# Two of eight batches transposed by TensorE instead of the DMA crossbar, and one expert's weights moved in the load queue

## The chip, the cores and the metric

The kernel runs on one core of a Trainium2 chip. The metric is the device time of one execution in microseconds (us); the times of several executions are given by their median. PE is TensorE's matmul stream and PEld its weight loads; DVE is VectorE, ACT ScalarE, POOL GpSimd, SP SyncE. Every engine works through its own list of instructions in a fixed order and waits, where it must, on semaphores of others. DMA transfers are issued from the queues of POOL, SP and ACT and land later.

## The reference, cut to what matters

```python
# attention: x (8, 8, 512, 64), state (8, 8, 32, 64); batch, head, tokens, width
scores  = scale * x @ state^T          # 512 x 32 for each batch and head
xread   = softmax(scores) @ state
scores2 = scale * state @ x^T          # the same products, the other way round
sread   = softmax(scores2) @ x
attn    = concat([xread, sread], axis=2)          # 544 rows for each batch and head
x       = attn with the heads side by side        # 4352 rows x 512

# mixture of 8 experts, every row through every expert
P = exp(x @ w_gate - max); 8 times: rows normalised, columns normalised, * N / E
out = sum over e of P[:, e] * (relu(x @ w1[e]) @ w2[e])   # w1: 512 x 1024, w2: 1024 x 512
```

Inputs and output are 32-bit floats. The kernel loads `x` and the weights into 16-bit tiles on the way.

## The kernel before, in words

**Two parts.** The first part holds attention for all eight batches, expert 0, the routing (the eight normalisations of P) and the first two blocks of expert 1's first layer. In it, every piece of work is an `op` with a rank, the engines that may run it with their costs, what it comes after, and the buffers that it takes or uses. `issue` (L48) walks through them: again and again it takes the ready op that could start earliest by these costs, then the one of lowest rank, and emits it. So the order of each engine's instructions is fixed when the program is built, from the costs written in the ops; on the chip each engine keeps to it. What `after` names serves this order; on the chip an instruction waits for data and buffers. The second part, the loop over experts 1 to 7 (`layer1`, `layer2`, L226 to L317), is written out in a fixed order.

**Attention, batch by batch.** The input of batch `b` is loaded by two POOL DMAs of 256 KB (L380) into `x_nat`, tokens on partitions; four such buffers rotate, so the load of batch 4 waits until batch 0's is done with. Scores need the input with the width on partitions: `xT`, 16 blocks of 128 x 128 per batch, three buffers. Two crossbar transposes per batch, issued by SP (L457), make it, one for the first four heads and one for the others. A batch then runs in two halves `q` of four heads. For each: PE's scores into the PSUM tile `psB` (L469; there is one such pair of banks, so the next scores wait until it is read); on DVE a flip of it into `eA` (L490), maxima, subtraction; on ACT two exponentials; on DVE sums and products; at last a flip into `aT` (L528), the attention weights that all experts read. Beside it PE transposes the other softmax (L547), that is copied to `ETs`, and PE reads the input with it (`su_ps`, L562). With that read, the `x_nat` buffer comes free.

**Expert 0.** Its two weight matrices are loaded by POOL, two DMAs of 512 KB each (L434). For each batch PE projects the state with w1 into `V` (L662), multiplies `V` by `aT` for the hidden layer (`hps`, L684; needs both halves' `aT`), ReLU goes to ACT or DVE (`hT`, L350 and L352), and PE runs the second layer (`yps`, L719). All of this is interleaved with attention by the planner. Six PSUM banks rotate among transposes, projections, hidden blocks and outputs.

**Routing.** After the last batch's logits, PE and DVE alternate: DVE normalises rows (L624 to L628), PE sums columns (`csb_ps`, L641), DVE normalises columns (L634 to L636). PE's list has expert 0's remaining work between the column sums.

**Queues around the change.** POOL issues, in this order: the identity matrices, then the loads: x 0, expert 0's w1, x 1, expert 0's w2, x 2, x 3, x 4, expert 1's w1, x 5, expert 1's w2, x 6, x 7, later the weights of the experts from 2 on (L166, L168). SP issues half of the state loads, the gate weights, and the 16 crossbar transposes in order of batches. `make_identity` stands twice for the 16-bit identity `identh`. The first PE instructions are 16 transposes of the states (`stT_ps`, L399), then 64 small matmuls for the gate (`G_ps`, L414), then batch 0's scores.

Of the kernel before, what the change touches and what calls it, by code (L numbers as in the profile page):

```python
# [10 lines left out]
FP16 = mybir.dt.float16  # L11
# [78 lines left out]
def kernel(  # L90
# [9 lines left out]
    nc = tc.nc  # L100
# [10 lines left out]
    NSC = S // 128  # L111
    NP = H // 2
    NQ = NP // 2
    NX = B * S
    NJ = NFB // 2
    DH = Dm // 2
# [3 lines left out]

    blocks = [(b * S, S) for b in range(B)] + [(NX, B * Ns)]

# [9 lines left out]
    def bank(shape, dtype, name, tag="bank"):  # L132
        return pools[tag].tile(shape, dtype, name=name, tag=tag)

    aT = persist.tile([128, B, NQ, S], FP16, name="aT")
    xsT = persist.tile([128, NKC, B * Ns], FP16, name="xsT")
# [2 lines left out]
    Pmat = persist.tile([128, NTB, E], FP32, name="Pmat")  # L139

    identh = persist.tile([128, 128], FP16, name="identh")
    make_identity(nc, identh)
    ident32 = persist.tile([128, 128], FP32, name="ident32")
    ones128 = persist.tile([128, 128], FP32, name="ones128")
    wg_st = persist.tile([128, NKC, E], FP32, name="wg_st")
    wgh = persist.tile([128, NKC, E], FP16, name="wgh")
    stT = persist.tile([128, B, NQ, 128], FP16, name="stT")
    G = persist.tile([128, B, NQ, E], FP16, name="G")

# [42 lines left out]
    def project(e, bi):  # L192
        if bi == B:
            return
        w1h = w16[e][0]
        V = vpool.tile([128, NQ, F], FP16, name="V", tag="V")
        vt[(e, bi)] = V
        for f in range(F // 512):
            cols = ds(f * 512, 512)
            ps = [bank([128, 512], FP32, "v_ps", ring[0]) for _ in range(NQ)]  # L200
            for j in range(4):
                for q in range(NQ):
                    r = ((j ^ q) % 2) * 64
# [117 lines left out]
    due_x = lambda u: 6.0 + 4.4 * u  # L321
    due_e = lambda bi: 14.0 + 13.0 * bi
    due_1 = 135.0
    rings = {"bank": Ring(6), "pair": Ring(1)}
    SHY = 0.8
    EVICT16 = {"DVE": (0.34, 0.48), "ACT": (0.48, 0.66)}
# [3 lines left out]
    def op(rank, on, emit, after=(), takes=(), uses=(), also=()):  # L330
        o = Op(rank, on, emit, after, takes, uses, also)
        ops.append(o)
        return o

    def slot(pool, n, shape, dtype, tag):
        return Slot(rings.setdefault(tag, Ring(n)),
                    lambda: pool.tile(shape, dtype, name=tag, tag=tag))

    def psum(shape, dtype, name):
        return Slot(rings["bank"], lambda: bank(shape, dtype, name))  # L340

    def copy(eng, out, in_):
        if eng == "ACT":
            nc.scalar.copy(out=out, in_=in_)
        else:
            engines[eng].tensor_copy(out=out, in_=in_)
# [7 lines left out]
    def dma(rank, kb, emit, after=(), takes=(), uses=(), also=()):  # L354
        return op(rank, {"DMA": (kb / 300.0, kb / 300.0 + 2.2)}, lambda _: emit(), after, takes, uses, also)
# [15 lines left out]
    wgc = op((10.0,), {"DVE": (0.15, 0.25)}, lambda _: nc.vector.tensor_copy(out=wgh, in_=wg_st), [wgd])  # L371


    make_identity(nc, identh)
    xn = [slot(axp, 4, [128, H, NSC * D], FP16, "x_nat") for _ in range(B)]
    x_ready = []
    for b in range(B):
# [5 lines left out]

        x_ready.append(dma((0, 1 + 2 * b), 1024, load, takes=[xn[b]], also={"POOL": 2.0}))

    make32 = op((8.0,), {"POOL": (0.5, 0.6)}, lambda _: make_identity(nc, ident32))
    bd = []
    for s_ in range(2):
# [4 lines left out]
    stT_ready = []  # L393
    for g in range(4):
        ps = psum([128, 4, 128], FP16, "stT_ps")

        def turn(_, g=g, ps=ps):
            for i in range(4):
                nc.tensor.transpose(ps.tile[:, i], st_in[:, 2 * g + i // 2, i % 2].rearrange("p s d -> p (s d)"),  # L399
                                    identh)  # L400

        def keep(eng, g=g, ps=ps):
            copy(eng, stT[:, ds(2 * g, 2)].rearrange("p b q c -> p (b q) c"), ps.tile)

        t = op((0, 1, g), {"PE": (0.35, 0.55)}, turn, bd, [ps])
        stT_ready.append(op((0, 1, g), EVICT16, keep, [t], uses=[ps]))
    gps = [psum([128, B, E], FP32, "G_ps") for _ in range(NQ)]

    def gmul(_):
        for b in range(B):  # L410
            for j in range(4):
                for q in range(NQ):
# [6 lines left out]
                  lambda eng, q=q: copy(eng, G[:, :, q], gps[q].tile), [gm_op], uses=[gps[q]])  # L419
# [4 lines left out]
    w_ready = {}  # L424
    t_ready = []

    def weights_ops(e, rank):
        w1 = slot(mw, 2, [128, NKC, F], FP16, "w1h")
        w2 = slot(mw, 2, [128, NFB, Dm], FP16, "w2h")
        wslots[e] = (w1, w2)  # L430
        for k, (w, n, r) in enumerate(((w1, 2, w1r), (w2, NJ, w2r))):
            def load(w=w, n=n, r=r):
                for g in range(2):
                    nc.gpsimd.dma_start(out=w.tile[:, ds(g * n, n), :], in_=r[e, :, ds(g * n, n), :])  # L434

            w_ready[e, k] = dma(rank[k], 2048, load, [], [w], [], {"POOL": 2.0})

    def w1_ready(e):
        return [w_ready[e, 0]]
# [1 line left out]
    def w2_ready(e):  # L441
        return [w_ready[e, 1]]

    weights_ops(0, [(0, 2), (0, 4)])
    weights_ops(1, [(due_1 - 60.0, k) for k in range(2)])


    a_ready, su_ready, gates = {}, [], []
# [3 lines left out]
    for b in range(B):  # L452
        xT = slot(axt, 3, [128, H * NSC // 2, 128], FP16, "xT")
        xt_ready = []
        for g in range(2):
            def turn(b=b, g=g, xT=xT):
                nc.sync.dma_start_transpose(out=xT.tile[:, ds(8 * g, 8), :],  # L457
                                            in_=xn[b].tile[:, ds(4 * g, 4), :].rearrange("p h c -> p (h c)"))

            xt_ready.append(op((due_x(2 * b - 2), 0, g), {"XBAR": (1.4, 3.0)}, lambda _, turn=turn: turn(),  # L460
                               [x_ready[b]], [] if g else [xT], [xn[b]] + ([xT] if g else [])))
        for q in range(NQ):
            r = lambda n, b=b, q=q: (due_x(2 * b + q) + 0.1 * 5.54 * n,)
            ps = Slot(rings["pair"], lambda: bank([128, 2, 512], FP32, "psB", "pair"))
# [12 lines left out]
            def tokens(t):  # L477
                return t.rearrange("p (i s c) -> p i s c", i=2, s=2)

            o2 = op((due_x(2 * b + q), 0), {"PE": (0.18, 0.38)}, score, [xt_ready[q]] + stT_ready,  # L480
                    [ps], [xT])
            mxA, sA, rA = rows("mxA"), rows("sA"), rows("rA")
            nmB, nsB, rowsum, rrec = small("nmB"), small("nsB"), small("rowsum"), small("rrec")
# [86 lines left out]

            u = op(r(9), {"PE": (0.25, 0.45)}, read, [k2], [su], [ETs, xn[b]])
            su_ready.append(op(r(9), {"DVE": (0.13, 0.25), "ACT": (0.15, 0.30)}, keepS, [u], [], [su]))

    def gate_op(bi, after):
        t0, tn = blocks[bi]
        n = tn // 128
        ps = psum([128, 4, E], FP32, "gate_ps")

        def mul(_):
            for i in range(n):  # L580
                rs = ds(i * 128, 128)
                if bi < B:
                    terms = [(aT[:, bi, q, rs], G[:, bi, q]) for q in range(NQ)]
                else:
                    terms = [(xsT[:, kc, rs], wgh[:, kc, :]) for kc in range(NKC)]
                for k, (lhs, rhs) in enumerate(terms):
                    nc.tensor.matmul(ps.tile[:, i], lhs, rhs, start=(k == 0),
                                     stop=(k == len(terms) - 1))

        t = op((due_x(2 * bi + 2), 0), {"PE": (0.25, 0.45)}, mul, after + G_ready, [ps])  # L590
        return op((due_x(2 * bi + 2), 0), {"DVE": (0.10, 0.20), "ACT": (0.15, 0.30)},
                  lambda eng: copy(eng, logits[:, ds(t0 // 128, n)], ps.tile[:, :n]), [t], [], [ps])
# [5 lines left out]
    rank = (-1.0,)  # L598
# [93 lines left out]
    for bi in range(len(blocks)):  # L692
# [6 lines left out]
        for fb in range(NFB):  # L699
            ps = psum([128, 512], FP32, "hps")  # L700
# [8 lines left out]
            t = op((due_e(bi) + 0.05 * 13.7 * fb,), {"PE": (0.44, 0.62)}, mul, deps, [ps], held)  # L709
# [48 lines left out]
    for bi in range(2):  # L758
# [12 lines left out]
        for j in range(NJ):  # L771
            for i in range(2):
                ps = psum([128, S], FP32, "hps")
# [7 lines left out]
                t = op((due_1 + 5.0 * bi, 1, j, i), {"PE": (0.44, 0.62)}, mul, deps + [got], [ps], held)  # L781
# [91 lines left out]
```

## Time and profile before

| | |
|---|---|
| median of 3 runs | 788.36 us (787.72 to 788.41) |
| profiled execution, its own time | 788.79 us |
| its span | 786.8 us |
| PE busy | 749.1 us, 95% of the span |
| DVE busy | 632.1 us, 80% |
| ACT busy | 524.0 us, 67% |
| POOL busy | 36.8 us, 5% |
| software DMA queue (POOL's loads) | 20.97 MB |
| hardware DMA queue (transposes, output, states) | 13.39 MB |

The span is the time from the first to the last instruction in the trace; the execution's own time has 2.0 us around it. "Busy" is the time in which an engine had an instruction running; matmuls are pipelined, so one that takes 379 ns by its row can start 107 or 213 ns after the one before. A line of the timeline gives start and duration in us, engine, line of the kernel, operation, what is written from what, how many instructions are merged in it, and in square brackets how long the engine stood idle before and who released it. Line numbers in profile lines are those of the kernel before.

### The profile page before, as it was taken

The numbers are of one execution on the slowest core, as the hardware profiler recorded it, in microseconds if no ns is written. First come the engines' busy times: TensorE is split into PE (matmuls) and PEld (weight loads), VectorE is DVE, ScalarE is ACT, GpSimd is POOL, SyncE is SP. The second block draws the span as 40 slices with busy tenths as digits, with TensorE's granted clock in tenths as the row PEclk, the third lists the DMA queues.
The fourth block names the chain that finished last, engine by engine and source line by source line (L and its number), as shares of the span: only waits on it lengthen the run. The fifth ranks groups of instructions, "written<-read, shape, count | busy, mean of one in ns | idle before, by whom it ended". The sixth has DMA issues, their size and how long they took to land.

```text
span 786.8 us, 16245 instructions
## 1 busy us (share of the span) xinstructions
PE 749.1 (95%) x6529; PEld 499.6 (64%) x6529; DVE 632.1 (80%) x1561; ACT 524.0 (67%) x1020; POOL 36.8 (5%) x58
## 2 busy tenths in 40 slices
PE   1699999989999999999999999999999999999996
PEld 1244444556667667766677667766677667766775
DVE  1699977678898888878888888878888888878885
ACT  1687787677767666576657666576667666576662
POOL 5111000100001000010001000010001000000000
PEclk9999999999999999999999999999999999999999
DMA  9999200330004100060004100060004200012223
GB/s 164 186 124 178 21 1 1 56 54 1 1 1 79 31 1 2 1 108 2 1 1 77 33 1 2 1 108 2 1 1 75 35 1 1 2 44 93 94 101 128
DMA packets 45916, 35.67 MB, mean 45 GB/s; under 512 B 21008, under 2 KB 37392, under 8 KB 45840
## 3 DMA queue, kind: packets, MB, share of 16 engines
q0 software_dynamic: 21248, 20.97, 18.1%
q1 hardware_dynamic: 23504, 13.39, 8.6%
q8 instruction: 51, 0.84, 0.4%
q10 hardware_dynamic: 1088, 0.26, 0.2%
q14 instruction: 25, 0.20, 0.1%
HBM read 42.48 MB, written 8.91 MB: 65 GB/s over the span
## 4 chain that ended last, share of the span: by engine, by line
PE 66%; DVE 4%; ACT 1%; issue 0%; DVEq 0%
PE hps L219 23%; PE Bseed L265 17%; PE E L265 11%; PE A L265 11%; PE v_ps L204 3%; DVE acc L279 2%; DVE sm L244 1%; ACT Hm L238 1%; DVE sm L247 0%; DVE Hm L245 0%; DVE T L178 0%; DVE sm L246 0%; DVE acc L287 0%; ACT Bseed L290 0%; DVEq L279 0%
## 5 line engine op out<-in xcount | busy, mean ns | idle before, releaser
L238 ACT ACTIVATE Hm<-hps 128x512 f16<-128x512 f32 (+1 forms) x488 | 261.6, 572 | 182.4 <-PE hps L219 167.3
L265 PEld LDWEIGHTS <-Hm 128*128 128x128 f16 x1904 | 186.1, 98 | 72.0 <-issue 4.1
L219 PE MATMUL hps<-aT,V 128*128 128x512 f16 x864 | 230.6, 379 | 0.0
L279 DVE SCALAR_TENSOR_TENSOR acc<-Bseed,Pmat,acc 128x256 f32<-128x256 f32 x357 | 156.9, 479 | 55.6 <-PE Bseed L265 52.9
L265 PEld LDWEIGHTS <-sm 128*128 128x128 f16 x1428 | 134.3, 98 | 53.1 <-DVE sm L244 24.4
L265 PE MATMUL A<-w2h,Hm 128*128 128x256 f16 x952 | 124.5, 273 | 1.9 <-ACT Hm L350 1.9
L265 PE MATMUL Bseed<-T,Hm 128*128 128x256 f16 x952 | 124.5, 273 | 1.0 <-DVE acc L279 0.8
L219 PEld LDWEIGHTS <-V 128*128 128x128 f16 x864 | 84.5, 98 | 44.5
L208 ACT CAST V<-v_ps 128x512 f16<-128x512 f32 x216 | 111.2, 609 | 0.0
L279 DVE SCALAR_TENSOR_TENSOR acc<-E,Pmat,acc 128x256 f32<-128x256 f32 x238 | 104.3, 477 | 5.2 <-PE E L265 0.9
L719 PE MATMUL yps<-w2h,hT 128*128 128x512 f16 x272 | 67.3, 386 | 0.0
L244 DVE TENSOR_TENSOR sm<-Hm 128x512 f16<-128x512 f16 (+1 forms) x122 | 49.9, 409 | 19.7 <-ACT Hm L238 18.9
L265 PE MATMUL E<-T,sm 128*128 128x256 f16 x476 | 64.4, 274 | 0.7
L279 DVE SCALAR_TENSOR_TENSOR acc<-A,Pmat,acc 128x256 f32<-128x256 f32 x119 | 52.3, 479 | 15.0 <-PE A L265 14.9
L265 PE MATMUL Bseed<-T,sm 128*128 128x256 f16 x476 | 62.4, 273 | 0.4 <-ACT Bseed L290 0.4
L265 PE MATMUL E<-w2h,sm 128*128 128x256 f16 x476 | 62.3, 273 | 0.0
L245 DVE TENSOR_TENSOR Hm<-Hm 128x512 f16<-128x512 f16 (+1 forms) x122 | 50.0, 410 | 4.2
L247 DVE TENSOR_TENSOR sm<-Hm,sm 128x512 f16<-128x512 f16 (+1 forms) x122 | 50.0, 410 | 4.2
L246 DVE TENSOR_TENSOR sm<-sm,Hm 128x512 f16<-128x512 f16 (+1 forms) x122 | 49.1, 402 | 0.0
L290 ACT COPY Bseed<-A 128x512 f32<-128x512 f32 (+1 forms) x63 | 34.5, 548 | 19.5 <-PE A L265 18.9
L719 PEld LDWEIGHTS <-hT 128*128 128x128 f16 x272 | 24.9, 100 | 26.8 <-issue 2.9
L684 PE MATMUL hps<-aT,V 128*128 128x512 f16 x160 | 41.0, 393 | 0.4 <-DVE aT L528 0.4
(100 smaller groups left out, 511.9 us busy)
## 6 DMA issues: line engine op xcount, KB each, us to landing
w1h<-in_moe_w_dram POOLq DMA_DIRECT2D x16, 512.0 KB, 7.1
w2h<-in_moe_w_dram POOLq DMA_DIRECT2D x16, 512.0 KB, 8.3
out_dram<-acc SPq DMA_DIRECT2D x32, 256.0 KB, 2.8
x_nat<-in_x_dram POOLq DMA_DIRECT2D x16, 256.0 KB, 11.9
out_dram<-acc SPq DMA_DIRECT2D x8, 64.0 KB, 1.7
st_st<-in_state_dram ACTq DMA_DIRECT2D x4, 64.0 KB, 3.0
st_st<-in_state_dram SPq DMA_DIRECT2D x4, 64.0 KB, 2.8
xT<-x_nat SPq DMA_TRANSPOSE x16, 12.0
```

Of the source, the lines that this page charges most:

```text
L208: nc.scalar.copy(out=V[:, q, cols], in_=ps[q])
L219: nc.tensor.matmul(out, lhs, rhs, start=(k == 0), stop=(k == len(terms) - 1))
L238: nc.scalar.activation(out=Hm[:, i, j, :tn], in_=hps[:, :tn], func=AF.Relu)
L244: nc.vector.tensor_add(s1, a21, a22)
L245: nc.vector.tensor_sub(a21, a11, a21)
L246: nc.vector.tensor_sub(s2, s1, a11)
L247: nc.vector.tensor_sub(s4, a12, s2)
L265: nc.tensor.matmul(dst[:, c], lhs(j, c), rhs[:, j], start=first and c == 0 and j == 0, stop=(j == NJ - 1), skip_group_check=True)
L279: nc.vector.scalar_tensor_tensor(out=dst, in0=src[:, c], scalar=p[:, k], in1=dst, op0=ALU.mult, op1=ALU.add)
L290: nc.scalar.copy(out=Bb[:, :nk], in_=A[:, :nk])
L684: nc.tensor.matmul(ps.tile[:, :tn], lhs, rhs, start=(k == 0), stop=(k == len(terms) - 1))
L719: nc.tensor.matmul(yps.tile, hT[fb].tile[:, ds(tk * 128, 128)], w2h[:, fb, :], start=(fb == 0), stop=(fb == NFB - 1))
```

## The change

Batches 0 and 1 (`NT = 2`) get their `xT` from PE. For each half of four heads, eight matmuls against the identity transpose 128 x 128 blocks into a PSUM bank, and two copies of 128 x 512 take it to SBUF, on DVE or ACT as the planner chooses. Batches 2 to 7 keep the crossbar; its cost in the planner goes from (1.4, 3.0) to (2.4, 6.0). One of the two `identh` identities goes, and the other becomes an op. Expert 1's weight loads are declared after the scores' transposes of the last batch (`last_x`). Built, the program has them on POOL's queue behind the load of x 7, with no further wait on the transposes; the loads of x 4 to x 7 move up.

```diff
+    NT = 2
 ...
-    make_identity(nc, identh)
 ...
-    make_identity(nc, identh)
 ...
+    makeh = op((0, 1.5), {"POOL": (0.5, 0.6)}, lambda _: make_identity(nc, identh))
 ...
-        t = op((0, 1, g), {"PE": (0.35, 0.55)}, turn, bd, [ps])
+        t = op((0, 1, g), {"PE": (0.35, 0.55)}, turn, bd + [makeh], [ps])
 ...
-            w_ready[e, k] = dma(rank[k], 2048, load, [], [w], [], {"POOL": 2.0})
+            w_ready[e, k] = dma(rank[k], 2048, load, last_x if e else [], [w], [], {"POOL": 2.0})
 ...
-    weights_ops(1, [(due_1 - 60.0, k) for k in range(2)])
 ...
-        for g in range(2):
+        for g in range(2 if b < NT else 0):
+            ps = psum([128, 8, 128], FP16, "xT_ps")
+
+            def turnX(_, b=b, g=g, ps=ps):
+                for k in range(8):
+                    nc.tensor.transpose(ps.tile[:, k], xn[b].tile[:, 4 * g + k // 2, ds((k % 2) * 128, 128)],
+                                        identh)
+
+            def keepX(eng, g=g, k=0, ps=ps, xT=xT):
+                copy(eng, xT.tile[:, ds(8 * g + 4 * k, 4), :], ps.tile[:, ds(4 * k, 4), :])
+
+            t = op((due_x(2 * b + g) - 2.0, 0), {"PE": (0.68, 0.85)}, turnX, [x_ready[b], makeh], [ps], [xn[b]])
+            xt_ready.append([op((due_x(2 * b + g) - 2.0, 0), EVICT16, lambda eng, k=k, keepX=keepX: keepX(eng, k=k), [t],
+                                [] if g + k else [xT], [ps] + ([xT] if g + k else [])) for k in range(2)])
+        for g in range(0 if b < NT else 2):
             def turn(b=b, g=g, xT=xT):
                 nc.sync.dma_start_transpose(out=xT.tile[:, ds(8 * g, 8), :],
                                             in_=xn[b].tile[:, ds(4 * g, 4), :].rearrange("p h c -> p (h c)"))
 
-            xt_ready.append(op((due_x(2 * b - 2), 0, g), {"XBAR": (1.4, 3.0)}, lambda _, turn=turn: turn(),
-                               [x_ready[b]], [] if g else [xT], [xn[b]] + ([xT] if g else [])))
+            xt_ready.append([op((due_x(2 * b - 2), 0, g), {"XBAR": (2.4, 6.0)}, lambda _, turn=turn: turn(),
+                                [x_ready[b]], [] if g else [xT], [xn[b]] + ([xT] if g else []))])
 ...
-            o2 = op((due_x(2 * b + q), 0), {"PE": (0.18, 0.38)}, score, [xt_ready[q]] + stT_ready,
+            o2 = op((due_x(2 * b + q), 0), {"PE": (0.18, 0.38)}, score, xt_ready[q] + stT_ready,
                     [ps], [xT])
 ...
+    last_x = xt_ready[0] + xt_ready[1]
+    weights_ops(1, [(due_1 - 60.0, k) for k in range(2)])
```

In the changed program the first PE instructions are the 16 state transposes, 16 transposes of batch 0, the gate's 64 small matmuls, both scores of batch 0, and batch 1's 16 transposes behind 32 of the first 48 V matmuls. SP has 12 crossbar transposes.

## The prediction

> **What bounds the kernel now.** I read the page first (span, shares in 40 slices), then the busy time by stage, then the waits up to 150 us, then the timeline of the first 40 us, because the edit touches only work of that stretch.
>
> From the page, then the table by stage (stretch, its length, busy time of PE, PEld, DVE, ACT, POOL with instruction counts, granted clock, DMA share, GB/s):
>
> ```profile
> span 786.8 us, 16245 instructions
> ...
> PE   1699999989999999999999999999999999999996
> DVE  1699977678898888878888888878888888878885
> ...
> 0.00:26.40 26.40, 3.86 (x108) 2.90 (x109) 6.41 (x16) 3.83 (x6) 10.69 (x22) 1.00 1.14 167
> 26.40:34.30 7.90, 6.46 (x94) 2.76 (x94) 7.27 (x18) 7.82 (x17) 0.60 (x1) 1.00 1.35 185
> 39.40:112.00 72.60, 69.30 (x709) 32.10 (x707) 68.90 (x161) 59.27 (x130) 5.95 (x8) 0.98 0.84 88
> 112.00:162.00 50.00, 49.80 (x331) 24.83 (x325) 32.12 (x88) 35.67 (x73) 2.88 (x4) 1.00 0.25 41
> ```
>
> PE is busy 69.30 of 72.60 us and 49.80 of 50.00 us in the two long stretches up to 162 us, where the experts' loop begins; behind that it stays near full. So PE carries the end, and its one large hole is the first 26.4 us: 3.86 us busy, 22.5 us idle. From 39.36 us (first second-layer matmul of expert 0) to the end PE's stream has hardly a gap: whatever moves that instruction moves the end.
>
> What fills the hole, from the waits (who, for whom: us in total, times, longest) and the timeline (start, duration):
>
> ```profile
> PE psB L469 <- DMA xT<-x_nat: 13.5, 2, 7.0
> ...
> 7.63 22.70 SPq L457 DMA_TRANSPOSE xT<-x_nat  x5
> 8.39 1.89 PE L399 MATMUL stT_ps<-identh,st_in 128*128 128x128 f16 x16 [8.39 <-ACT st_in L344]
> ...
> 18.57 0.41 PE L469 MATMUL psB<-xT,stT 64*32 64x256 f16 x8 [7.05 <-DMA xT<-x_nat]
> ...
> 25.49 0.41 PE L469 MATMUL psB<-xT,stT 64*32 64x256 f16 x8 [6.50 <-DMA xT<-x_nat]
> 25.98 0.72 DVE L490 STREAM_TRANSPOSE eA<-psB 128x512 f32<-128x512 f32 x1 [3.52 <-PE psB L469]
> 26.37 1.48 PE L662 MATMUL v_ps<-w1h,stT 64*32 64x512 f16 x24
> ...
> 34.33 1.44 PE L684 MATMUL hps<-aT,V 128*128 128x512 f16 x3 [0.39 <-DVE aT L528]
> ...
> 39.36 1.89 PE L719 MATMUL yps<-w2h,hT 128*128 128x512 f16 x8
> ```
>
> The two scores of batch 0 wait 7.05 and 6.50 us for the crossbar; no later score waits for it. Its first two transposes are issued at 7.63 and 9.6 us and land 10.9 and 15.8 us later. The V projections (L662) stand behind them in PE's order, and the first hidden layer (L684) needs both heads' aT, the second of which ends at 34.28 us.
>
> **The change, part by part.** Counts and order of the changed program are read from its instruction streams; durations from rows of before.
>
> *Batch 0's transposes to PE.* 16 transposes directly behind the 16 of the states. Nearest row: L399, 16 in 1.89 us (118 ns each). From 10.28 they end at 12.17; the input landed at 7.6 and 9.0 us (issue 2.39 and 3.3, landing 5.2 and 5.7 later). Four copies out of PSUM, two on DVE (row 424 ns) and two on ACT (row 594 ns), the last ending near 12.9; G's 64 small matmuls (0.65 us) fit beside. First score: about 12.9 instead of 18.57, gain 5.65 us; its flip on DVE 13.4. Bounds for 16 transposes: 1.6 us (later E transposes, 4 in 0.40) to 2.4 us (16 x the 152 ns weight load of L399); I take L399's row, which has the same shape in the same place, so +-0.5 us.
>
> *The second score.* Both halves are now on chip, so it waits only for the first exponential to release the pair bank: in before that ends 2.8 us after the first flip. Flip of the second score: DVE is free 3.4 us after the first flip (19.05 to 22.45 before), so 16.8 instead of 25.98: gain 9.2 us.
>
> *Batch 1's transposes to PE.* They stand behind 32 of the first 48 V matmuls (16 x 118 ns = 1.9 us). PE is not the limit there: V's 12 copies on ACT at 626 ns pace it. What they cost lies on ACT and DVE, between the second flip (16.8) and its aT. Before, that took 8.3 us (25.98 to 34.28). Now one xT copy on ACT stands ahead of the second eA exponential (+0.6); the ETs copy has gone to DVE behind the two xT copies (+0.4; the xT copies themselves lie in DVE's wait for eA); the next head's flip and max stand ahead of aT (about 1.25 by starts in the timeline). 8.3 + 2.25 = 10.55: aT at 27.35 instead of 34.28, gain 6.9. Bounds: none of the extras shows (gain 9.2), or all count twice (4.65).
>
> *First hidden layer.* In before one of its eight ReLUs ran on DVE; now all eight are on ACT behind the last V copies: +0.6 (row 598 ns). L719 at about 33.0 instead of 39.36: **gain 6.3 us**. Expert 0's weights landed at 12.2, 15.1 (w1) and 22.7, 26.5 us (w2), ahead of their first uses at 17.4 and 33.0.
>
> *Crossbar.* 4 of 16 transposes leave the queue and 12 go on. Batch 2's score stands behind 28 of batch 0's 32 second-layer matmuls, about 41 us. In before its input landed at 28.7 and 30.8 us and its transposes 7.3 and 6.7 later, at 36.0 and 37.5: in time even if the emptier queues bring nothing. Cost 0; if that cover is gone, PE waits there next. Batch 3's and 4's transposes now also wait for PE's reads of the xT buffers of batches 0 and 1 and for ACT's copies into them, past by then.
>
> *Expert 1's weights.* On POOL's queue four DMAs leave their places behind batches 4 and 5 and stand behind batch 7's load. Nothing in the instruction waits for the last transposes; only the queue order moved. Batch 7's load was issued at 69.44; 6.3 earlier plus its own 1.5 and the four issues' 2.9 gives about 67.5 for the last, and 18.3 (the slowest landing of these weights) 86 us. First readers: the T subtractions at 117.12 and V at 153.09, 6.3 earlier. Slack 25 us: cost 0. Batches 4 to 7 lose that company in the queue, but no score waited there: gain 0. Behind these on POOL come only expert 2's loads, held by PE until 149.88.
>
> *One identity fewer on POOL* (0.20 + 0.29 us rows): loads issue about 0.6 us earlier. PE reads nothing of them before 10.28, so 0.
>
> *Order.* The planner's new transpose costs reshuffle PE: up to the routing's first transpose it now places 180 second-layer and 112 V matmuls instead of 172 and 96, same total, so about 2.5 us more work before the routing and less behind it. Between two column sums of the routing PE has 3.4 us of work or more, as before, where DVE waited for PE each time (0.54 to 1.4 us). Cost 0.
>
> **Sum.** Profiled execution 788.79 us (span 786.8 and 2.0 around it) - 6.3 = 782.5. The median is 0.43 below that execution: **782.1 us**. With the bounds (gain 9.2; 4.65 less 0.6 = 4.05): 779.2 to 784.3.
>
> [...] The row: crossbar transposes of 256 KB landed after 10.9 and 15.8 us, copies of the same size after 5.2 and 5.7. [...]
>
> **The rivals.**
> 1. *Batch 2 becomes the new wait.* For it: the slowest crossbar landing of the trace is 17.2 us; 28.7 + 17.2 = 45.9, 4.7 us behind 41.2. Then 782.1 + 4.7 = 786.8. Against: its own two took 7.3 and 6.7, with more traffic beside them. Chance 0.11.
> 2. *The early start is swallowed by DVE:* attention runs at DVE's pace (68.90 of 72.60 us), and PE, starting sooner, waits later. Time about 788. For it: the extra 2.5 us of PE work and 16 units of some 5.3 us on DVE. Against: DVE moves 6 us earlier too (the third batch's flip from 46.90 to about 41), and 50 us of PE work without a gap stand behind attention. Chance 0.08. A crossbar landing as fast as the copies' 5.2 to 5.7 us leaves nothing to gain either (788); the rows speak against it: 0.01.
> 3. *Slower: the clock.* PE's weight loads take 152 ns until about 37.5 us and 98 after; and the table of 90 to 100 us shows a granted clock of 0.83, 0.53 in 93 to 96: some 3.4 us at half speed, 1.7 us lost, in a stretch where PE waits for DVE. If the earlier start thins PE's work between 30 and 110 us, such windows multiply. The gain is gone with the fourth extra one (6.8 us), and it is slower from the fifth: 788.36 - 6.3 + 8.5 = 790.6. Against: one window in 72 us now, and the same work. [...] Chance 0.06.
> 4. *More than forecast:* the dip does not recur and half of the 2.85 us of extras hides: 782.1 - 1.7 - 1.4 = 779.0. Chance 0.06.
>
> **How the numbers follow.** Forecast 0.68 (779.2 to 784.3), rivals 0.11, 0.08 + 0.01, 0.06, 0.06. 0.2% is 1.6 us, about what a measurement tells from no change. Faster: 0.68 + 0.06 + 0.09 of rival 1 (its stall can be shorter) = 0.83; same 0.11; slower 0.06. Range: rivals 2 and 3 (0.15) lie above, a little of 4 below: 779.2 to 787.0.
>
> **What would show it.** First score near 13 us and second flip near 17; 32 transposes at about 118 ns; first L684 pair complete near 27 and the second layer's first matmul near 33; the experts' loop from about 155.7 instead of 162. Wrong: a PE wait for the crossbar at batch 2 (rival 1), PE idle growing between 33 and 112 us (rival 2), granted clock below 1 in more slices (rival 3).

## The result and the profile after

The changed kernel takes 777.18 us (median; 776.96 to 778.15) against 788.38 us: ratio 0.9862, 95% interval 0.9845 to 0.9879. It is 11.2 us faster, where 6.3 us were forecast; the time lies below the stated range (779.2 to 787.0). In a later group the same kernel had a median of 778.0 us beside 788.57.

From the page after, and from the table by stage (the third stretch of the table before; the columns are the stretch, its length, and the busy times of PE, PEld, DVE, ACT, POOL):

```profile
span 775.3 us, 16309 instructions
...
PE   3899999899999999999999999999999999999996
...
39.40:112.00 72.60, 72.20 (x733) 33.70 (x733) 66.89 (x160) 61.54 (x133) 7.33 (x10) 1.00 0.52 74
```

The first two slices of PE have risen, as forecast, from 1 and 6 tenths to 3 and 8. But 39.40 to 112.00 us has changed too: PE is busy 72.20 us of it, against 69.30 before, at a clock of 1.00 against 0.98. That was not forecast.

The start in the timeline after (start, duration, and in brackets the idle time before):

```profile
9.63 1.89 PE L399 MATMUL stT_ps<-identh,st_in 128*128 128x128 f16 x16 [9.63 <-ACT st_in L344]
...
11.31 1.91 PE L459 MATMUL xT_ps<-identh,x_nat 128*128 128x128 f16 x16
...
12.27 0.18 DVE L371 CAST wgh<-wg_st 128x32 f16<-128x32 f32 x1 [0.29 <-DMA wg_st<-in_moe_w_gate_dram]
...
13.63 0.45 PE L482 MATMUL psB<-xT,stT 64*32 64x256 f16 x8
...
17.46 0.72 DVE L503 STREAM_TRANSPOSE eA<-psB 128x512 f32<-128x512 f32 x1
...
27.13 0.69 DVE L541 STREAM_TRANSPOSE aT<-a 128x512 f16<-128x512 f16 x1
...
33.53 1.89 PE L735 MATMUL yps<-w2h,hT 128*128 128x512 f16 x8
```

From the first score on everything runs as laid out in the forecast, 0.5 to 0.7 us later; the second layer's first matmul is at 33.53 us (forecast 33.0). PE's first instruction is later by more: 9.63 us, where the forecast took 8.39 from before. What was not forecast comes behind it. I call the time from that matmul to the first of the experts' loop *the stretch*. The table by stage for the stretch, before and then after:

```profile
39.36:161.99 122.63, 119.13 (x1028) 56.97 (x1027) 101.05 (x249) 94.96 (x202) 8.83 (x12) 0.99 0.60 69
```

```profile
33.53:150.70 117.17, 116.58 (x1018) 55.83 (x1016) 98.92 (x243) 92.40 (x198) 10.21 (x14) 1.00 0.46 71
```

So of the 11.68 us between the two profiled executions (788.79 and 777.11), 5.83 are won ahead of the stretch and 5.46 in it (122.63 - 117.17). The loop takes 624.8 and 624.6 us (span less its start), and 0.2 us is outside the span. Inside the stretch PE's idle time falls from 3.50 to 0.59 us and its busy time from 119.13 to 116.58. Most of the idle time before were waits in attention (PE's waits from 33 to 165 us: us in total, times, longest):

```profile
PE su_ps L562 <- ACT ETs L344: 1.1, 1, 1.1
PE su_ps L562 <- DVE ETs L346: 0.6, 1, 0.6
PE ET_ps L547 <- DVE E L516: 0.6, 2, 0.3
```

### The profile page after: what moved, and what is told of

Same layout as the page of the kernel before. It is cut to its first block, busy times and chain, and to the rows that moved or that the text cites. A ratio compares the mean times of both kernels' runs of the same rounds, so it can differ in the third digit from the quotient of the medians.

```text
span 775.3 us, 16309 instructions
## 1 busy us (share of the span) xinstructions
PE 748.8 (97%) x6561; PEld 501.1 (65%) x6561; DVE 634.6 (82%) x1566; ACT 524.8 (68%) x1023; POOL 36.2 (5%) x56
## 4 chain that ended last, share of the span: by engine, by line
PE 67%; DVE 4%; ACT 1%; issue 0%; DVEq 0%
PE hps L219 23%; PE Bseed L265 17%; PE E L265 12%; PE A L265 11%; PE v_ps L204 3%; DVE acc L279 2%; DVE sm L244 1%; ACT Hm L238 1%; DVE Hm L245 0%; DVE sm L247 0%; DVE T L178 0%; DVE sm L246 0%; DVE acc L287 0%; ACT Bseed L290 0%; DVEq L279 0%
## 5 line engine op out<-in xcount | busy, mean ns | idle before, releaser
L735 PE MATMUL yps<-w2h,hT 128*128 128x512 f16 x272 | 65.4, 380 | 0.0
```

Of the source, the lines that this page charges most:

```text
L735: nc.tensor.matmul(yps.tile, hT[fb].tile[:, ds(tk * 128, 128)], w2h[:, fb, :], start=(fb == 0), stop=(fb == NFB - 1))
```

## The experiments

"First L719" is always the first second-layer matmul, whatever its line number in that kernel.

**1 and 2. Is it the weight loads?** Two kernels move only them; neither changes the order on PE, DVE or ACT.

```diff
  # changed kernel, weights back
     weights_ops(0, [(0, 2), (0, 4)])
+    weights_ops(1, [(due_1 - 60.0, k) for k in range(2)])
 ...
-    last_x = xt_ready[0] + xt_ready[1]
-    weights_ops(1, [(due_1 - 60.0, k) for k in range(2)])
```

> The changed kernel with expert 1's weight loads back in their old places on POOL's queue (behind the loads of batches 4 and 5); the order on PE, DVE and ACT is unchanged by it. Four theories for the 5.5 us that the stretch from the first second-layer matmul to the experts' loop lost (122.6 to 117.2 us). Queue theory (the weights delayed the batches' inputs and transposes, and PE paid): the stretch grows back by 3 to 5 us, 780 to 782 us. Order theory (the planner's new order of PE), head-start theory (attention starts earlier and PE stops waiting for DVE) and clock theory (one window of half clock lay in that stretch before and lies ahead of it now): stretch stays at 117, 777.2 +- 0.5 us.

```diff
  # kernel before, weights moved
-    weights_ops(1, [(due_1 - 60.0, k) for k in range(2)])
 ...
+    last_x = xt_ready
+    weights_ops(1, [(due_1 - 60.0, k) for k in range(2)])
```

> The kernel before with only expert 1's weight loads moved behind batch 7's load; the order on PE, DVE and ACT is that of before. Queue theory: 783 to 785 us. Order, head-start and clock theories: 788.4 +- 0.5 us.

Measured: 778.18 us (778.03 to 778.49), and 788.14 us (ratio 0.9995, interval 0.9986 to 1.0005). The stretch of the first is 117.21 us, the same as the changed kernel's; its first score is 0.8 us later, which the seventh run explains. The queue theory falls: the move alone is worth nothing that these runs can tell.

The second shows the clock instead. Its stretch, in the order of before:

```profile
40.37:161.32 120.95, 117.42 (x1028) 56.45 (x1027) 100.47 (x249) 94.50 (x201) 10.22 (x14) 1.00 0.44 67
```

1.7 us shorter than before's 122.63, with the same idle time (3.53). In the profile before, the granted clock in the stretch falls to half for 3.4 us, from 92.4 to 95.8 (the row begins 0.2 us late, so its mean is 0.53):

```profile
92.60:96.00 3.40, 3.40 (x20) 1.47 (x12) 3.33 (x11) 1.22 (x2) 0.00 (x0) 0.53 0.02 5
```

Half clock for 3.4 us cost 1.7 us in this stretch. In this run, and in the changed kernel, the half-clock window lies ahead of the stretch (here at 33.2 to 40.0 us, in the changed kernel at 28.7 to 32.1). There it is not free: in this run first L719 comes 1.0 us later than before (40.37 against 39.36), and the profiled execution is only 0.7 us shorter (788.10 against 788.79).

**3. Does the end follow the start?**

```diff
  # changed kernel; copies on ACT (s_ = 0) seven times
-            copy(eng, st_in[:, :, :, s_, :], st_st)
+            for _ in range(1 if s_ else 7):
+                copy(eng, st_in[:, :, :, s_, :], st_st)
```

> The changed kernel with ACT's cast of the states run seven times instead of once (6.2 us more in front of PE's first instruction), the same order on PE and DVE, loads as they were. The prediction's step that a shift of the start moves the end by as much: 777.2 + 6.2 = 783.4 us, stretch 117. If waits for loads or transposes still decide anything behind the start, less than that: 779 to 782. Clock theory alone: the half-clock window may fall into the stretch again, then 785.

Measured: 784.04 us, 6.0 to 6.9 above the changed kernel's medians of 778.0 and 777.18; stretch 117.19 us. The end follows the start, and the stretch does not depend on how far the loads are ahead.

**4. The early start in the order of before.**

```diff
  # kernel before; at the planner's places for batch 0's crossbar transposes
+                if b < 1:
+                    pt = bank([128, 16, 128], FP16, "xT_ps", "pair") if not g else head[0]
+                    head[:] = [pt]
+                    for k in range(8):
+                        nc.tensor.transpose(pt[:, 8 * g + k], ..., identh)
+                    for k in range(2):
+                        copy(("DVE", "ACT")[k], xT.tile[:, ds(8 * g + 4 * k, 4), :], ...)
+                    return
```

> The kernel before with batch 0's two crossbar transposes replaced by 16 PE transposes and four copies at the very places where the planner of before emits them; everything else keeps the order of before, batch 1 stays on the crossbar. First score near 14 us. Order theory: the stretch stays near 122, the end comes 5 to 6 us earlier, 782 to 784 us. Head-start theory: the stretch shrinks too, 777 to 779 us. If batch 1's crossbar transposes become the wait: 784 to 787 us.

Measured: 784.92 us, with an uncommonly wide spread (780.81 to 788.55); the profiled execution is the fastest of them. There, first L719 at 33.30 us and the stretch:

```profile
33.30:154.31 121.01, 117.52 (x1028) 56.32 (x1027) 100.58 (x249) 94.74 (x202) 8.82 (x12) 1.00 0.58 75
```

The start has moved by 6 us, the stretch has the length and the 3.49 us of idle time of the order of before at full clock. Head start does not shorten it. PE's longest wait on a transfer in that start is 1.6 us, for batch 1's crossbar; the median lies in the range expected for a longer such wait, but what made the other executions slower no profile shows.

**5 and 6. Which edit makes the order?** The planner's cost of a crossbar transpose alone, in the kernel before and taken back in the changed one:

```diff
  # 5: kernel before          # 6: changed kernel, the reverse
-{"XBAR": (1.4, 3.0)}
+{"XBAR": (2.4, 6.0)}
```

> The kernel before with only the planner's cost of a crossbar transpose changed to (2.4, 6.0): the same instructions, another order. Order theory, cost alone: the stretch from the first second-layer matmul to the experts' loop is 117 to 118.5 us with PE idle under 1.5 us in it, 783 to 786 us. If the order that pays needs the transposes on PE in the plan: stretch 121 to 122.6, idle 3.5 us, 787.5 to 789 us.

> The changed kernel with the planner's old crossbar cost (1.4, 3.0): the order differs from the third batch's scores on. Order theory, cost alone: the stretch grows back to 120 to 121 us, 780.5 to 781.5 us. If the transposes on PE make the order: 117 to 118 us, 777 to 778 us.

Measured: 5: 787.41 us (ratio 0.9982, interval 0.9972 to 0.9992); 6: 783.96 us (0.9942, interval 0.9921 to 0.9964). The stretches:

```profile
41.53:159.73 118.20, 116.36 (x1019) 56.37 (x1017) 99.66 (x243) 93.88 (x203) 8.81 (x12) 1.00 0.49 67
```

```profile
33.99:156.28 122.29, 116.83 (x1018) 56.41 (x1016) 98.32 (x239) 92.49 (x202) 10.22 (x14) 1.00 0.42 68
```

In 5 the new order shortens the stretch to 118.20 (1.84 us idle), but starts it at 41.53 us instead of 39.36, so the time hardly gains: ahead of the stretch PE waits 3.16 us to transpose a second softmax and 1.24 us for the first hidden layer. In 6 the start is nearly as early as in the changed kernel (33.99), but PE is idle 5.46 us in the stretch, which is longer than either theory expected. With all its PE transposes and the old cost the change is worth 4.6 us; the number (2.4, 6.0), which no instruction carries, is worth another 6 to 7 us beside them, and 1.2 us without them (run 5). Who waits in 6, and in the changed kernel, in PE's waits from 30 to 165 us:

```profile
PE su_ps L575 <- ACT ETs L344: 3.0, 3, 1.1
PE ET_ps L560 <- DVE E L529: 1.2, 3, 0.6
PE psB L482 <- ACT E L521: 0.8, 2, 0.6
```

```profile
PE ET_ps L560 <- DVE E L529: 0.3, 2, 0.2
```

Beside these, both have one wait of 1.9 us in the loop. No line names the crossbar in either. PE waits for attention's own chain on DVE and ACT: in that order the work of expert 0 put between a score and what follows it is used up before the chain has answered. The tenth run comes back to this with a count.

**7. The identity, and the start itself.** Beside another run of the changed kernel, one with the second identity back on POOL:

```diff
-    makeh = op((0, 1.5), {"POOL": (0.5, 0.6)}, lambda _: make_identity(nc, identh))
+    makeh = op((0, 1.5), {"POOL": (0.5, 0.6)},
+               lambda _: [make_identity(nc, identh) for _ in range(2)])
```

> The changed kernel itself, to stand beside the others of this group: 777.2 +- 0.5 us. Its first score was at 13.6 us in one execution and at 14.4 in the run with the old weight places, and there the gate-weight cast in front of the copies on DVE waited for its 16 KB load 0.3 and 1.7 us. If the landing of that load varies from run to run, the time varies by about 1 us with it.

> The changed kernel with the second 16-bit identity back on POOL in front of the loads, so they are issued 0.6 us later, as before; order on PE, DVE and ACT unchanged. Theory that the earlier loads delay the states' loads (cast of the states at 7.23 us instead of 5.99, gate weights used at 12.3 instead of 10.7): first transposes 1.2 us earlier, near 8.4 us, 775.5 to 776.2 us. Theory that the states land later for another reason: 777.2 us.

Measured: 778.0 us (777.38 to 779.25) and **775.4 us** (775.38 to 777.4; ratio to before 0.984, interval 0.9817 to 0.9864). Doing the identity twice is 2.6 us faster than once beside it, and 1.8 faster than the changed kernel's first median (777.18). The timeline of the run with two, and of the other:

```profile
5.42 1.28 ACT L344 ACT_TABLE_LOAD   x1 [5.42 <-DMA st_st<-in_state_dram]
...
11.82 0.45 PE L482 MATMUL psB<-xT,stT 64*32 64x256 f16 x8
```

```profile
7.35 1.28 ACT L344 ACT_TABLE_LOAD   x1 [7.35 <-DMA st_st<-in_state_dram]
13.82 0.18 DVE L371 CAST wgh<-wg_st 128x32 f16<-128x32 f32 x1 [1.73 <-DMA wg_st<-in_moe_w_gate_dram]
```

With one identity POOL's loads are issued 0.6 us earlier; the states land up to 1.9 us later, and the 16 KB of gate weights land so late that their cast, which stands on DVE in front of the copies of `xT`, holds these up by 0.29 us in the first profile after and 1.73 in this one. That is the 0.8 us of the first run. Other profiles agree: with one identity the table load on ACT, which stands behind the states' loads, starts at 7.05 to 7.35 us (both profiles of the changed kernel, runs 1 and 6), and the gate weights take 8.8 and 10.4 us to land (those of the changed kernel); with two it starts at 5.42 to 5.99 us (before, run 4 and the run with two), and they take 4.2 to 4.4 (before, run 2 and the run with two). Why these small loads land so much later no run tells.

**8 and 9. Another order.** If PE idles for want of expert work between scores, any planner number that puts more of it there should do. The flip's cost on DVE raised, first with the old crossbar cost, then as a candidate with two identities and the new cost (both give the same order):

```diff
-            m0 = op(r(2), {"DVE": (0.60, 0.72)}, flip, [o2], [eA], [ps])
+            m0 = op(r(2), {"DVE": (1.20, 1.30)}, flip, [o2], [eA], [ps])
```

> The changed kernel with the old crossbar cost in the planner (1.4, 3.0), which gave 784.0 us and a stretch of 122.3 us with 5.5 us of PE idle, and with the planner's cost of the flip on DVE raised from 0.60 to 1.20 us: same instructions. The order then has 4.4 us of expert 0's matmuls per score from the fifth score on, where that kernel had 3.9 and the changed kernel 4.0 but with 1.7 us more already ahead of the fifth. Fill theory (PE idles where its list holds too little expert work between scores for DVE's pace, whatever made the order): stretch 117 to 118.5, idle under 1.5, 777 to 779 us. Crossbar theory (the new cost pays because it places the scores of batches 2 to 7 where their transposes have really landed): stretch 121 to 122.5, 783 to 784 us.

> The same order as the run with the raised flip cost, and the second identity back in front of the loads, which alone gave 775.4 us: a candidate to beat the changed kernel. Fill theory: 775 to 776.5 us, first score near 12 us, stretch 117 to 118.5. Crossbar theory: 781 to 782 us.

Measured: 784.16 and 778.62 us. The stretches, 124.18 (with a half-clock window of 6.8 us in it) and 121.30, are near what the crossbar theory said, but no PE wait names the crossbar; the fill theory missed. The second, its stretch, and its three waits above 0.15 us there (timeline):

```profile
31.58:152.88 121.30, 116.67 (x1018) 56.36 (x1016) 98.19 (x236) 94.90 (x208) 10.22 (x14) 1.00 0.50 74
```

```profile
44.38 0.43 PE L575 MATMUL su_ps<-ETs,x_nat 128*64 128x32 f16 x16 [1.40 <-ACT ETs L344]
...
108.16 0.33 PE L603 MATMUL gate_ps<-G,aT 128*128 128x8 f16 x7 [2.19 <-DVE aT L541]
...
146.19 0.36 PE L657 MATMUL csb_ps<-cpart,ones 128*128 128x8 f32 x2 [0.76 <-DVE cpart L644]
```

The small waits between 50 and 100 us are gone, as fill has it. But 1.40 us stays at the third batch, where this order has 2.6 us of expert work between the sixth score and the seventh, and the changed kernel's 5.1; 2.19 us are new at the end of attention, where PE has run out of other work and waits for `aT`; and 0.76 us lie in the routing. In the first of the two, the clock also falls to half between 110.8 and 117.6 us. More fill on the whole is not enough: it counts where it lies.

**10. Half of the transposes.**

```diff
-    NT = 2
+    NT = 1
```

> The changed kernel with only batch 0 on PE, batch 1 on the crossbar. Fill theory: its order has as much expert work ahead of the scores as the changed kernel's from the sixth on, stretch 117 to 118.5; the start is later by what batch 1's crossbar costs, 0 to 3 us: 777 to 781 us, and it varies from run to run as the landing does.

Measured: 779.68 us (779.06 to 781.79). First L719 at 32.43 us, no later than with two batches on PE; stretch 121.55 with 2.97 us idle and, inside it, a half-clock window at 44.8 to 48.2 us. The expected stretch was wrong: its order has 1.3 us of expert work between the fifth and sixth scores, where the changed kernel's has 3.4, and 2.1 between the fifteenth and sixteenth, where that has 3.8; there PE waits 1.43 and 1.23 us, and nowhere else before the routing.

Counted so, score by score, the traces show what decides. From the fifth score to the sixteenth, the orders of before, after and runs 5, 6, 9 and 10 have 66 intervals from one score to the next. In nine of them PE's list has 2.6 us of expert 0's matmuls or less, and PE waits in all nine, 0.30 to 1.52 us. In the other 57 it has 3.0 or more, and PE waits in four, by 0.56 us at most. The changed kernel has none of the nine, before has three, runs 6 and 10 two each, 5 and 9 one each. (Counted in the timelines: hidden and second-layer matmuls by 213 ns, where the timeline after shows 216 from start to start, eight in 1.89 us with the last taking 0.38; V's by 51, eight in 0.41 us; waits from 0.15 us. No run moves a single interval alone.)

**11. The order of after with the crossbar of before.** The transposes of batches 0 and 1 and their eight copies are left out of PE, DVE and ACT and go through the crossbar:

```diff
             def turnX(_, b=b, g=g, ps=ps):
-                for k in range(8):
-                    nc.tensor.transpose(...)
+                pass
 ...
             def keepX(eng, g=g, k=0, ps=ps, xT=xT, b=b):
-                copy(eng, xT.tile[:, ds(8 * g + 4 * k, 4), :], ps.tile[:, ds(4 * k, 4), :])
+                if not k:
+                    nc.sync.dma_start_transpose(out=xT.tile[:, ds(8 * g, 8), :], in_=...)
```

> The mirror of the run with the order of before: the changed kernel's order on every engine, but the transposes of batches 0 and 1 go through the crossbar as before, at the places of the first copies; the 32 PE transposes and eight copies are left out. If order and transposes are two separate gains: first score near 18.5 us, first second-layer matmul at 39.5 to 41.5, stretch 117 to 118 with PE idle under 1 us, 782.5 to 785.5 us. If the order pays only together with the early start: stretch 120 to 122, idle 3 us or more, 786.5 to 789 us.

Measured: 786.3 us (784.76 to 788.06). First score at 18.4 us, first L719 at 41.78, and the stretch:

```profile
41.78:158.97 117.19, 116.58 (x1018) 55.89 (x1016) 98.69 (x243) 92.49 (x198) 10.21 (x14) 1.00 0.47 67
```

The stretch is the changed kernel's to 0.02 us. So it belongs to the order alone, early start or not. The time missed its expectation by 0.8 us: in this order first L719 comes 2.4 us later than before though the first score does not, and ahead of it PE waits 2.19 us to transpose a second softmax and 1.34 us for the first hidden layer.

## Why the prediction was wrong

**The start: right in its steps; that it is only 0.5 us off is partly luck.** Forecast 6.3 us ahead of first L719, measured 5.83. First score 13.63 instead of 12.9, second flip 17.46 instead of 16.8, second `aT` 27.82 instead of 27.35; batch 0's 16 transposes took 1.91 us (row taken: 1.89). The chain of extras between the flip and `aT` came to 10.4 us (forecast 10.55). Two errors offset each other: PE's first instruction came at 9.63 us, 1.24 later than forecast, because the states landed later (run 7); and from there first L719 took 23.9 us, where the forecast had 24.6.

**Where it went wrong: "Order ... Cost 0", and the rigid shift behind it.** The step said that PE's stream from 39.36 us on "has hardly a gap" and that a reshuffle of the same work costs nothing. The stretch had 3.50 us of PE idle time in view and one half-clock window that the forecast itself priced, and the new order removes the idle time. By terms, of the 5.46 us:
- idle time 2.9 us, by the order: run 11 has this gain without the early start, run 4 lacks it with one;
- the half-clock window 1.7 us: it lay at 92.4 to 95.8 us before and lies ahead of the stretch now. The same order without the window (runs 2 and 4) measures 120.95 and 121.01. The three such windows inside a stretch (before, runs 8 and 10) each begin close to a PE wait of over 1 us (1.10, 2.19 and 1.04); the changed order has no such wait there. But runs 2 and 4 have before's waits and no window, so whether an order lets PE's clock fall in a given place is not settled. Of the whole time this term is worth less than 1.7 us, as run 2 shows;
- about 0.7 us of work, one score (0.30) and one transposition of the second softmax (0.40), that the new order has placed ahead of first L719; this is moved, not saved.

The forecast read the counts before the routing (180 against 172 matmuls) as "more work before and less behind". Read per score they say more: ahead of the seventh score PE's list has 20.4 us of expert 0's matmuls in the changed kernel and 16.9 before, ahead of the ninth 28.5 and 25.0. From the fifth to the sixteenth score it is 44.3 and 39.6 us, and PE went through these eleven scores in 56.8 and 57.9 us. Such a mean does not yet decide: run 9 has 48.5 us there and still idles. The single intervals of the tenth run do: before has three short ones, after none. That count was open before the result; I had counted only DVE's share of the long stretch, and used it for rival 2.

**"One identity fewer ... 0" was a mis-sized term.** It costs 1.8 to 2.6 us (run 7). The step asked only who reads the loads that come earlier, not what lands later for it.

**Batch 2 and the crossbar (rival 1): right not to weigh.** No PE wait names the crossbar after; its median landing fell from 12.0 to 4.9 us with 12 transposes instead of 16, and that of `x_nat` from 11.9 to 6.4. The first two of before, with expert 0's weight loads beside them, landed 10.9 and 15.8 us after their issue.

**Expert 1's weights: cost 0, right** (runs 1 and 2). **Rivals 2 and 3** did not happen; that thinner work on PE brings half-clock windows, as rival 3 supposes, no run shows. **Rival 4** had the direction, and with 1.7 us the right price for the clock inside the stretch, but not the order; nor did the extras hide (10.4 us of 10.55). Its 779.0 us is 1.8 above the measured time.

## What to carry to other kernels

When a cost in a planner changes, the order of every engine is part of the change: count, interval by interval and not as a mean, how much independent work the bound engine holds between two steps of the slower chain; total idle time in a "full" stretch is what a better order can still win. A single number that no instruction carries was worth 6 to 7 us here beside the transposes moved to PE, and 1.2 without them. And loads that are issued earlier can make others land later (16 KB in 8.8 and 10.4 us here, instead of 4.4): look for the small one in front of the first instruction.

## What the runs showed that I had not expected

- The half-clock windows given above are 3.4 us long (before, after, run 10) or 6.8 (runs 2 and 8), and their place differs between kernels with the same order (92.4 us before, 33.2 in run 2) and between executions of one kernel (from 30 to 40 us the mean clock is 0.90 in the first profile after and 0.78 in the second); run 5 and run 11 show none in the stretch (1.00). The window of before followed 3.4 us in which PE was busy for 1.9 and paused for 1.1 at most. At the start the record of the granted clock is not the whole tale: in before most weight loads of 128 x 128 take about 150 ns until 37.5 us, as they do in its window, and 98 behind that, while the granted clock reads 1.00.
- A 16 KB load took 8.8 us to land (10.4 in the second profile) instead of 4.4 when the large loads were issued 0.6 us earlier, and decided the first score through the order on DVE.
- The best kernel of this study keeps the redundant identity: 775.4 us, 13 us below the kernel before.
